# Sliding-window attention with a two-layer MLP: tile 0's attention moved ahead of the weights, its masks added as scores on TensorE, its layer one in wide products

## The chip, the cores and the metric

The kernel runs on one core of a Trainium2 chip. A core has five engines with a queue of instructions each: TensorE (PE, matrix products and transposes into PSUM), VectorE (DVE), ScalarE (ACT), GpSimd (POOL) and SyncE (SP). Loads and stores run on 16 DMA engines; here POOL issues all loads, SP the stores and the transposes done by DMA. The metric is the device time of one execution in microseconds (us). "The profile" is one execution recorded instruction by instruction, with times from the span's start.

## The reference

```python
scores = scale * np.matmul(q, k.transpose(0, 1, 3, 2))     # 8 batches, 8 heads, 576 tokens, 64 wide
mask = np.abs(pos[:, None] - pos[None, :]) <= 32
scores = np.where(mask, scores, -1000000000.0)
attn = softmax(scores)                                     # over the last axis
x = (attn @ v) with the heads side by side                 # 4608 tokens x 512
h = x @ w_in                                               # w_in 512 x 2048
g = h * (1.0 / (1.0 + np.exp(-1.702 * h)))
out = g @ w_out                                            # w_out 2048 x 512, float32
```

Inputs are float32 in HBM; loads convert q, k, v to bf16 and the weights to f16.

## The kernel before, in words

The 4608 tokens are 36 units of 128 queries, and nine tiles of four units (512 tokens). Everything is written out in program order; nothing is scheduled by a planner. An engine runs its queue in that order, so a waiting instruction holds up what stands behind it.

Attention of a unit: `scores` (24 small products into two PSUM banks, then two exponentials on ACT, into p), `band` (L257, DVE multiplies p by a 0/1 mask), `values` (16 pairs of products p by v, with a column of ones that gives the sums), `norm` (DVE: reciprocal and product, giving x), `x_T` or `x_T2` (PE transposes x for one or two units, and a copy brings it to xT). The odd half-blocks of v lie shifted by 64 tokens in `vo`, which `odd_v` (L200) copies from two neighbouring `ve` tiles, two copies a unit.

Layer one of tile 0 is done directly by `layer1_plain` (L377), layer two by `layer2_plain` (64 products of 512 columns, handed out a few at a time by `do(self.l2, n)`). Tiles 1 to 8 use a Strassen-like scheme with seven products in place of eight (`l1_group`, `layer2`), fed by sums of weights (`w1_sums`, `w2_sums`), of x and of g that DVE makes.

`opening` (L561) is tile 0, and the attention of tile 1. It loads k and q of tile 0 in two parts (`load_first`, `T_first`), k and q of tile 1 together (`load_four`, `T_four`: 32 PE transposes and two copies each), v by units (`load_v`, unit 4 in two halves), w_in in four chunks of 512 columns (`load_w1`) and w_out in four chunks of 512 rows (`load_w2`). All of these are issues on POOL's queue, and the n-th waits on the semaphore of the load eight before it. The loads' order before: k and q part 0, v0 to v2, w_in 0, k and q part 1, w_in 1, v3, half of v4, w_in 2, half of v4, tile 1's k and q, w_in 3, v5, v6, w_out 0, v7, v8, w_out 1 to 3, then tile 2's loads (`fetch`).

PE's order before: units 0 and 1 with `keep_busy` (products on a zero tile whose results nobody reads) in between, then transposes of part 1 mixed with layer one on the first half of the tokens, units 2 and 3, more layer one, tile 1's transposes, scores and values of units 4 to 7 mixed with the rest of layer one and 24 of the layer-two products. After it come `x_sums(1)` and `first_layer1`, tile 1's layer one.

PSUM has eight banks, all named: A, C, B, E, LA, LB and the double bank t. Taking a bank waits until its last reader is done. ACT needs another table for exponentials than for the gelu; each switch is an `ACT_TABLE_LOAD`.

Of the kernel before, what the change touches and what calls it, by code (L numbers as in the profile page):

```python
# [22 lines left out]
SQ = 64  # L23
TILE = 512


class _Kernel:
# [7 lines left out]
    def __init__(self, ctx, tc, q, k, v, w_in, w_out, out):  # L35
# [18 lines left out]
        self.g, self.gs, self.o = {}, {}, {}  # L54
# [28 lines left out]
    def setup(self):  # L83
# [3 lines left out]
        self.mask = cst.tile([128, 4, SQ], BF16, name="mask")  # L87
        self.w1 = cst.tile([128, 4, self.DFF], F16, name="w1")
# [10 lines left out]
    def setup_mask(self):  # L99
        pool, m = self.nc.gpsimd, self.mask  # L100
        lo, hi = slice(0, 64), slice(64, 128)
        pool.memset(m, 1.0)
        for blks, rows, sign in ((slice(0, 2), lo, 1), (slice(0, 2), hi, -1), (slice(2, 4), lo, -1), (slice(2, 4), hi, 1)):
            ap = m[rows, blks, :]
            pool.affine_select(out=ap, in_=ap, compare_op=ALU.is_ge, fill=0.0, base=0,
                               pattern=[[0, 2], [-sign, SQ]], channel_multiplier=sign)

    def cut_mask(self):
        lo, hi = slice(0, 64), slice(64, 128)
        for b, rows, cols in ((0, hi, slice(0, 32)), (0, lo, slice(32, 64)), (2, lo, slice(0, 32)), (2, hi, slice(32, 64))):  # L110
            self.nc.gpsimd.memset(self.mask[rows, b, cols], 0.0)

    def load_w1(self, c, n=1):
        w = 512 * n
        self.nc.gpsimd.dma_start(self.w1[:, :, c * 512:c * 512 + w],  # L115
                                 self.w_in[:, c * 512:c * 512 + w].rearrange("(k p) f -> p k f", p=128))
# [39 lines left out]
    def T_first(self, c, part, tags, engs):  # L156
# [6 lines left out]
        for i, (tag, eng) in enumerate(zip(tags, engs)):  # L163
            tp = self.bank(tag, [128, 2, j, n // j], BF16, "tp")
            for h in range(4):
                for x in range(j):
                    self.nc.tensor.transpose(tp[64 * (h % 2):64 * (h % 2) + 64, h // 2, x, :],
                                             src[:, 4 * i + h, at + x, :], self.ident[r, r])
            self.copy(eng, dst[:, 2 * i:2 * i + 2, :].rearrange("x h (p j) -> x h p j", j=j),
                      tp.rearrange("x h j p -> x h p j"))  # L170
# [66 lines left out]
    def scores(self, u, tag):  # L237
        kT, q = self.kT[u], self.qT[u]
        nxt = self.k_first if u == self.NU - 1 else self.kT[u + 1][:, :, 0:64]
        if tag == "t":  # L240
            sc = self.bank(tag, name="sc")
            sc = [sc[:, 0], sc[:, 1]]
        else:
            sc = [self.bank(x, name="sc") for x in tag]
        for hp in range(4):
            c = 128 * hp
            for eo in range(2):
                r = slice(64 * eo, 64 * eo + 64)
                lo, hi = sc[eo][0:64], sc[eo][64:128]
                self.mm(lo[:, c:c + 64], kT[r, hp, 0:64], q[r, hp, 0:64], start=(hp == 0))  # L250
                self.mm(hi[:, c:c + 128], kT[r, hp, 64:128], q[r, hp, :], start=(hp == 0))
# [125 lines left out]
    def layer1_plain(self, t, d, half, tag, later=None):  # L377
# [3 lines left out]
        c = slice(256 * half, 256 * half + 256)  # L381
        for i in range(2):
            f = 2 * d + i
            for kr in range(4):
                self.mm(h[:, 256 * i:256 * i + 256], self.w1[:, kr, 128 * f:128 * f + 128], self.xT[t][:, kr, c],
                        start=(i == 0 and kr == 0))

        def gelu():
            self.nc.scalar.activation(g[:, 2 * d:2 * d + 2, c], h.rearrange("p (i n) -> p i n", i=2),
                                      AF.Gelu_apprx_sigmoid)  # L390
# [170 lines left out]
    def opening(self):  # L561

        nc, dve, act, pool = self.nc, self.nc.vector, self.nc.scalar, self.nc.gpsimd
        self.setup()
        dve.memset(self.idle, 0.0)
        dve.memset(self.spark, 0.0)
        for t in self.ve:
            dve.memset(t[:, :, self.D:], 1.0)
        self.load_first("k", 0)
        self.load_first("q", 0)  # L570
        make_identity(nc, self.ident)
        act.activation(self.spark, self.spark, AF.Exp)
        for u in (0, 1, 2):
            self.load_v(u)
        self.load_w1(0)
        self.setup_mask()
        self.load_first("k", 1)
        self.load_first("q", 1)
        self.cut_mask()
        self.load_w1(1)  # L580
        self.load_v(3)
        self.load_v(4, slice(0, 1))
        self.load_w1(2)
        self.load_v(4, slice(1, 2))
        self.load_four("k")
        self.load_four("q")
        self.load_w1(3)
        dve.tensor_copy(self.identh, self.ident)
        self.keep_busy(10, "E", 512)
        self.T_first("k", 0, "AC", (dve, act))  # L590
        self.keep_busy(2, "E", 512)
        self.T_first("q", 0, ("LA", "LB"), (dve, act))
        self.keep_busy(1, "E", 512)
        for u in (5, 6):
            self.load_v(u)
        self.load_w2(0)
        for u in (7, 8):
            self.load_v(u)
        for c in (1, 2, 3):
            self.load_w2(c)  # L600
        self.load_kq("k", 8)
        self.scores(0, "t")
        self.scores(1, "AC")
        self.odd_v(0, dve)
        self.odd_v(1, dve)
        self.keep_busy(4, "E", 512)
        self.band(0)
        self.values(0, "t")
        self.band(1)
        self.norm(0)  # L610
        self.values(1, "AC")
        self.norm(1)
        self.keep_busy(2, "E", 512)
        self.x_T(0, "LA", act)
        self.keep_busy(1, "E", 512)
        self.x_T(1, "LB", act)
        self.T_first("k", 1, "AC", (dve, dve))
        h, n, gelus = [], [0], []

        def l1(half, *ds):  # L620
            for d in ds:
                self.layer1_plain(0, d, half, h[n[0] % len(h)])
                n[0] += 1

        self.layer1_plain(0, 0, 0, "B", gelus)
        self.T_first("q", 1, ("LA", "LB"), (dve, act))
        self.layer1_plain(0, 1, 0, "E", gelus)
        self.odd_v(2, dve)
        self.odd_v(3, dve, (0,))
        h[:] = ["B", "E", "LA", "LB"]  # L630
# [281 lines left out]
```

## Time and profile before

| what | us |
|---|---|
| median of 3 runs (285.96 to 287.16) | 287.05 |
| the profiled execution itself | 285.75 |
| its span, first to last instruction | 284.0 |
| PE busy in the span | 272.8 (96%) |
| DVE busy | 217.2 (76%) |
| ACT busy | 193.9 (68%) |
| POOL busy | 126.9 (45%) |

Rows of the profile give engine, line, operation, output<-input with shapes, and count. A busy PE is not always a useful one: products on the zero tile count as busy. Names in rows: `w` is w_in or w_out in SBUF, `h` layer one's result in PSUM, `o` layer two's, `sc` scores, `pv` values, `tp` a transpose in PSUM, `kq` the k and q of tile 0 or their transposes, `o_sb<-in_k_dram` the k of tile 1 (its buffer is shared with later outputs), `ve` and `vo` the v blocks, `junk` the products on zeros. Line 70 is the helper through which all products go.

### The profile page before, as it was taken

To read this page: it belongs to the slowest core of one execution; us is meant where nothing else is said; L and a number is where in the kernel's file an instruction comes from. 1 tells how busy PE (TensorE), PEld (TensorE's weight loads), DVE (VectorE), ACT (ScalarE), POOL (GpSimd) and SP (SyncE) were. 2 spreads that over 40 slices of the span, in tenths; PEclk is the share of its full clock that TensorE was granted. 3 is DMA by queue.
4 is the path that set the end of the run, shared out by engine and by line. 5 is a ranking of instruction groups with operands and counts; after the bars stand their busy time and mean duration, and the time that the engine had idled before them with its cause. 6 is when DMAs were issued, how large, how long until landed. Compare 5 with 4: busy or idle time off the path is not lost.

```text
span 284.0 us, 8953 instructions
## 1 busy us (share of the span) xinstructions
PE 272.8 (96%) x3684; PEld 223.3 (79%) x3684; DVE 217.2 (76%) x501; ACT 193.9 (68%) x340; POOL 126.9 (45%) x192
## 2 busy tenths in 40 slices
PE   6787999999999998999999999999999999999995
PEld 2466847776778887888888888888888888888884
DVE  1754997898887877798879887878788878946731
ACT  2556684799886778667966796689658875568411
POOL 8975446898599726739083909340110000000000
PEclk9999999999999999999999999999999999999999
DMA  8999999999999999999999999995422030201024
GB/s 90 182 193 196 184 204 159 193 124 147 136 154 152 200 127 195 124 203 143 201 102 189 131 203 82 198 146 140 132 58 71 26 113 14 81 2 74 2 95 133
DMA packets 149610, 37.63 MB, mean 132 GB/s; under 512 B 138048, under 2 KB 145216, under 8 KB 149568
## 3 DMA queue, kind: packets, MB, share of 16 engines
q0 software_dynamic: 106000, 18.42, 95.0%
q1 hardware_dynamic: 43120, 18.10, 34.2%
q8 instruction: 29, 0.48, 0.7%
q10 hardware_dynamic: 448, 0.52, 0.6%
q14 instruction: 13, 0.11, 0.1%
HBM read 36.83 MB, written 9.44 MB: 163 GB/s over the span
## 4 chain that ended last, share of the span: by engine, by line
PE 82%; DMA 7%; DVE 5%; POOL 4%; issue 1%; ACT 0%; DVEq 0%; POOLq 0%
PE o L70 37%; PE h L70 36%; PE pv L70 4%; DMA w<-in_moe_w_in_dram 4%; DMA xT<-x 3%; PE sc L70 3%; POOL ve L198 1%; POOL kq L142 1%; DVE xs L353 1%; DVE vo L209 1%; PE tp L321 1%; PE tp L231 1%; DVE a L334 1%; PE tp L188 1%; POOL w L115 1%
## 5 line engine op out<-in xcount | busy, mean ns | idle before, releaser
L418 ACT ACTIVATE g<-h 128x512 f16<-128x512 f32 x128 | 72.2, 598 | 35.7 <-PE h L70 34.9
L70 PEld LDWEIGHTS <-g 128*128 128x128 f16 x576 | 54.4, 98 | 9.5
L70 PEld LDWEIGHTS <-a 128*128 128x128 f16 x512 | 49.1, 97 | 12.3 <-DVE xs L353 2.2
L70 PE MATMUL h<-xs,a 128*128 128x256 f16 x384 | 57.6, 272 | 0.9 <-DVE xs L353 0.7
L70 PE MATMUL o<-w,g 128*128 128x256 f16 (+1 forms) x320 | 55.5, 294 | 0.0
L70 PEld LDWEIGHTS <-w 128*128 128x128 f16 x512 | 48.9, 98 | 8.4 <-DMA w<-in_moe_w_in_dram 1.7
L70 PE MATMUL h<-xT,w 128*128 128x256 f16 x384 | 54.0, 273 | 1.4 <-DMA w<-in_moe_w_in_dram 1.4
L209 POOL COPY vo<-ve 64x264 int32<-64x264 int32 x55 | 25.5, 463 | 61.3 <-PE pv L70 59.0
L70 PEld LDWEIGHTS <-gs 128*128 128x128 f16 x384 | 36.8, 98 | 4.7
L255 ACT ACTIVATE p<-sc 128x512 bf16<-128x512 f32 x72 | 36.9, 620 | 2.6 <-PE sc L70 2.5
L70 PE MATMUL o<-b,gs 128*128 128x256 f16 x256 | 37.6, 273 | 0.0
L70 PE MATMUL o<-b,g 128*128 128x256 f16 x256 | 37.5, 273 | 0.0
L198 POOL DMA_DIRECT2D ve<-in_v_dram x40 | 34.4, 865 | 6.2 <-DMA qst<-in_q_dram 2.8
L431 DVE TENSOR_TENSOR h<-h,s 128x512 f32<-128x512 f32 x32 | 22.3, 698 | 17.8 <-PE h L70 17.5
L131 POOL DMA_DIRECT2D qst<-in_q_dram x35 | 28.1, 804 | 3.5 <-DMA w<-in_moe_w_out_dram 2.8
L67 ACT COPY h<-h 128x512 f32<-128x512 f32 x32 | 18.9, 589 | 15.5 <-PE h L70 15.1
L293 DVE TENSOR_TENSOR x<-pv,rec 128x256 f16<-128x256 f32 (+1 forms) x53 | 27.6, 520 | 1.8
L131 POOL DMA_DIRECT2D kst<-in_k_dram x31 | 26.4, 855 | 5.0 <-DMA ve<-in_v_dram 2.6
L437 DVE TENSOR_TENSOR h<-h,s 128x512 f32<-128x512 f32 x32 | 22.4, 700 | 4.6 <-PE h L70 3.9
L263 DVE TENSOR_TENSOR p<-p,mask 128x1024 bf16<-128x1024 bf16 x36 | 25.0, 698 | 0.8 <-ACT p L255 0.6
L67 ACT COPY s<-h 128x512 f32<-128x512 f32 x32 | 19.2, 599 | 2.0 <-PE h L70 0.7
L70 PE MATMUL h<-xs,w 128*128 128x256 f16 x128 | 19.2, 273 | 0.0
(83 smaller groups left out, 343.7 us busy)
## 6 DMA issues: line engine op xcount, KB each, us to landing
out_dram<-o_sb SPq DMA_DIRECT2D x33, 256.0 KB, 4.6
ve<-in_v_dram POOLq DMA_DIRECT2D x32, 128.0 KB, 6.6
kst<-in_k_dram POOLq DMA_DIRECT2D x25, 128.0 KB, 6.6
qst<-in_q_dram POOLq DMA_DIRECT2D x21, 128.0 KB, 6.1
w<-in_moe_w_in_dram POOLq DMA_DIRECT2D x4, 512.0 KB, 8.9
w<-in_moe_w_out_dram POOLq DMA_DIRECT2D x4, 512.0 KB, 12.6
qst<-in_q_dram POOLq DMA_DIRECT2D x7, 96.0 KB, 6.4
kq<-in_q_dram POOLq DMA_DIRECT2D x2, 256.0 KB, 5.9
```

The source lines that it names most:

```text
L67: (eng.copy if eng is self.nc.scalar else eng.tensor_copy)(out, in_)
L70: self.nc.tensor.matmul(out, lhsT, rhs, start=start, stop=stop, skip_group_check=True)
L115: self.nc.gpsimd.dma_start(self.w1[:, :, c * 512:c * 512 + w], self.w_in[:, c * 512:c * 512 + w].rearrange("(k p) f -> p k f", p=128))
L131: self.nc.gpsimd.dma_start(t[off:off + n], src[b, :, s:s + n, :].rearrange("h s d -> s h d"))
L198: self.nc.gpsimd.dma_start(t[off:off + n, :, :self.D], self.v[b, :, s:s + n, :].rearrange("h s d -> s h d"))
L209: eng.tensor_copy(*((words(vo[64:128]), words(self.ve[u % 9][64:128])), (words(vo[0:64]), words(nxt)))[i])
L255: self.nc.scalar.activation(p[:, eo].rearrange("k h s -> k (h s)"), sc[eo], AF.Exp, scale=self.scale)
L263: (eng or self.nc.vector).tensor_mul(pv, pv, msk.to_broadcast([128, 8, 2, SQ]))
L293: dve.tensor_mul(x[:, 4 * at:4 * (at + n), :].rearrange("p (b h) d -> p b h d", b=n), acc[:, :, :, :D], r.to_broadcast([128, n, 4, D]))
L418: act.activation(g[:, f, 256 * half:256 * half + 256], bank.rearrange("p (i n) -> p i n", i=2), AF.Gelu_apprx_sigmoid)
L431: dve.tensor_add(e, b, s7)
L437: dve.tensor_add(c, b, s7)
```

## The change

Seven things, all but the last two in `opening`:

- The loads' order becomes k and q of tile 0 (both parts), v0 to v3, half of v4, w_in 0 and 1, then on POOL eight `odd_v` copies, then w_in 2, tile 1's k and q, w_in 3, the rest of v4, v5 to v8, w_out 0 to 3, eight more `odd_v` copies, and then tile 2's loads. The sixteen copies ran on DVE before.
- The identity matrices and the mask are made on DVE from one iota on POOL; they were made on POOL.
- For units 0 to 3, `seed` writes 0 or -1e8 into the two score banks by a product of the identity and a bias tile, and the score products add to it; the exponential then gives zero outside the band, and `band` is not called.
- Attention of units 0 to 3 is done whole before layer one begins. The zero products are 24 of 128 columns, 12 of 256, and 8 of 64, in place of 20 of 512.
- Layer one of tile 0 is done for two pairs of column blocks in halves of 256 tokens, for the other twelve blocks in products of 512 tokens. Two of these blocks are copied by DVE from PSUM to SBUF and their gelu taken from there; the gelus of blocks 10 to 15 are called after the exponentials of units 4 to 7. Again 24 of the layer-two products are called in `opening`, in groups of 4, 4, 8 and 8.
- Unit 10 and 11's transposes of x become two `x_T`, copied by DVE and ACT, instead of one `x_T2` copied by DVE.
- One `w1_sums` of the second half moves from `opening` into `first_layer1`.

```diff
...
     def setup_mask(self):
-        pool, m = self.nc.gpsimd, self.mask
-        lo, hi = slice(0, 64), slice(64, 128)
-        pool.memset(m, 1.0)
...
+        D = self.work.tile([128, 128], F32, name="gap", tag="s7", bufs=2)
+        self.nc.gpsimd.iota(D, pattern=[[-1, 128]], base=0, channel_multiplier=1,
+                            allow_small_or_imprecise_dtypes=True)
+        dve = self.nc.vector
+        dve.tensor_single_scalar(self.ident, D, 0.0, op=ALU.is_equal)
+        dve.tensor_copy(self.identh, self.ident)
...
+                dve.tensor_single_scalar(self.mask[r, blk:blk + 2, :], d, 0.0, op=op)
...
+    def setup_bias(self):
+        m = self.mask[:, 1:4:2, :].rearrange("p (o b) s -> p o b s", o=1).to_broadcast([128, 4, 2, SQ])
+        self.nc.vector.tensor_scalar(out=self.bias.rearrange("p (o b s) -> p o b s", o=4, b=2), in0=m, scalar1=-1.0,
+                                     scalar2=1.0e8, op0=ALU.add, op1=ALU.mult)
...
+    def seed(self, u, tag):
+        self.sc[u] = self.score_banks(tag)
+        for x in self.sc[u]:
+            self.mm(x, self.ident, self.bias, start=True)
...
+    def scores(self, u, tag=None):
...
+        bias = tag is None
+        sc = self.sc.pop(u) if bias else self.score_banks(tag)
         for hp in range(4):
             c = 128 * hp
+            start = hp == 0 and not bias
...
+    def layer1_plain(self, t, f, half, tag, later=None, eng=None):
...
+        fs, c = ((f, f + 1), slice(256 * half, 256 * half + 256)) if half is not None else ((f,), slice(0, TILE))
+        w = TILE // len(fs)
+        for i, f1 in enumerate(fs):
             for kr in range(4):
+                self.mm(h[:, w * i:w * i + w], self.w1[:, kr, 128 * f1:128 * f1 + 128], self.xT[t][:, kr, c],
                         start=(i == 0 and kr == 0))
+        if eng:
+            kept = self.sb("s7", [128, 512], F32, 2)
+            self.copy(eng, kept, h)
+            h = kept
...
```

The new body of `opening`, after the two loads of part 0 and the setup:

```python
self.load_first("k", 1); self.load_first("q", 1)
act.activation(self.spark, self.spark, AF.Exp)
for u in (0, 1, 2, 3): self.load_v(u)
self.load_v(4, slice(0, 1))
self.load_w1(0); self.load_w1(512)
for u in (0, 1, 2, 3): self.odd_v(u, pool)
self.load_w1(1024)
self.load_four("k"); self.load_four("q")
self.load_w1(1536)
self.load_v(4, slice(1, 2))
for u in (5, 6, 7, 8): self.load_v(u)
for c in range(4): self.load_w2(c)
self.keep_busy(24, "E", 128); self.keep_busy(12, "E")
self.T_first("k", 0, "AC", (dve, act)); self.seed(0, "t")
self.T_first("q", 0, ("LA", "LB"), (dve, act)); self.seed(1, "AC")
self.scores(0); self.scores(1)
self.T_first("k", 1, ("LA", "LB"), (dve, dve)); self.T_first("q", 1, ("B", "E"), (dve, act))
self.seed(2, "t"); self.seed(3, "AC")
self.keep_busy(8, "LA", 64)
self.scores(2); self.scores(3)
self.values(0, ("LA", "LB")); self.norm(0)
self.values(1, ("B", "E")); self.norm(1)
self.x_T(0, "LA", act)
self.values(2, "t"); self.norm(2)
self.x_T(1, "LB", act)
self.values(3, "AC"); self.norm(3)
self.x_T(2, "B", act)
h, n = ["LA", "LB", "A", "C", "B", "E"], [0]
l1(0, 0)
self.x_T(3, "E", dve)
l1(0, 2); l1(1, 0, 2)
...
l1(None, 4, 5, 6, 7, 8)
for i in (3, 1, 2, 4): self.w1_sums((i,), 0)
...
self.T_four("k", "BE", (dve, act))
...
l1(None, 9)
self.T_four("q", "BE", (dve, act))
for u in (4, 5, 6, 7): self.odd_v(u, pool)
self.load_kq("k", 8)
for u in (8, 9, 10, 11): self.fetch(u)
l1(None, 10, later=gelus, eng=dve)
self.scores(4, "AC"); self.scores(5, "t"); self.scores(6, "BE")
l1(None, 11, later=gelus, eng=dve)
self.scores(7, "AC"); self.band(4); self.band(5)
l1(None, 12, later=gelus); self.values(4, "t")
l1(None, 13, later=gelus); self.band(6); self.norm(4)
l1(None, 14, later=gelus); self.values(5, "AC"); self.band(7)
l1(None, 15, later=gelus); self.norm(5)
self.values(6, "t")
self.do(gelus[2:4] + gelus[0:2] + gelus[4:])
self.norm(6)
self.do(self.l2, 4)
self.values(7, "AC"); self.norm(7)
self.do(self.l2, 4)
self.x_T2(4, "t", act)
self.do(self.l2, 8)
self.x_T2(6, "A", dve)
self.do(self.l2, 8)
```

Later in `run` and in `first_layer1`:

```diff
-        self.x_T2(10, "C", dve)
+        self.x_T(10, "A", dve)
+        self.x_T(11, "C", act)
...
-        dv = [lambda i=i: self.w1_sums((i,), 1) for i in (1, 2, 4)]
+        dv = [lambda i=i: self.w1_sums((i,), 1) for i in (3, 1, 2, 4)]
```

More of the change, by code (lines that the diff above doesn't have):

```diff
@@ L87, in setup @@
         self.mask = cst.tile([128, 4, SQ], BF16, name="mask")
+        self.bias = cst.tile([128, 512], BF16, name="bias")
         self.w1 = cst.tile([128, 4, self.DFF], F16, name="w1")
@@ L564, in opening @@
         self.setup()
+        self.load_first("k", 0)
+        self.load_first("q", 0)
         dve.memset(self.idle, 0.0)
         dve.memset(self.spark, 0.0)
+        self.setup_mask()
+        self.cut_mask()
+        self.setup_bias()
         for t in self.ve:
             dve.memset(t[:, :, self.D:], 1.0)
[L569 to L574, printed above, removed]
@@ L592, in opening @@
         self.T_first("q", 0, ("LA", "LB"), (dve, act))
[L593 to L608, printed above, removed]
@@ L614, in opening @@
         self.x_T(0, "LA", act)
[L615 to L628, printed above, removed]
```

173 lines of the change are left out of this document (86 added, 87 removed).

## The prediction

> **What bounds the kernel now.** I read the view by slices first, then stretches of ten microseconds, then the timeline of the opening. From 50 us on, TensorE (PE) is busy without a break and the change hardly touches it, so the opening is what can move. In this table each row is a stretch, followed by the busy time of PE, weight load, VectorE (DVE), ScalarE (ACT), GpSimd (POOL), and at the end GB/s of DMA:
>
> ```profile
> 0.00:10.00 10.00, 7.51 (x121) 3.75 (x121) 3.11 (x17) 3.58 (x6) 8.55 (x19) 1.00 1.24 112
> 10.00:20.00 10.00, 7.82 (x153) 5.37 (x152) 6.32 (x15) 4.66 (x10) 8.02 (x15) 1.00 1.56 192
> 20.00:30.00 10.00, 8.12 (x124) 6.63 (x122) 6.25 (x15) 6.45 (x11) 5.61 (x7) 1.00 1.45 197
> 30.00:40.00 10.00, 9.55 (x206) 6.82 (x205) 9.30 (x18) 8.95 (x15) 5.04 (x8) 1.00 1.61 191
> 40.00:50.00 10.00, 9.98 (x102) 6.57 (x102) 8.32 (x22) 5.56 (x9) 6.12 (x8) 1.00 1.99 170
> ```
>
> PE idles 6.55 us in the first 30 us (2.49 + 2.18 + 1.88), and the groups add 6.8 us of products on the zero tile, which compute nothing. In the same time DMA runs at an even 190 to 200 GB/s: the loads are in one saturated stream, and each lands when all loads ahead of it have. The timeline shows when (start, length, work, and in brackets the wait before it):
>
> ```profile
> 1.27 3.78 PE L70 MATMUL junk<-idle 128*128 128x512 bf16 x10 [1.27 <-DVE spark L566]
> 6.81 0.60 PE L70 MATMUL junk<-idle 128*128 128x512 bf16 x2
> 23.44 1.05 PE L70 MATMUL h<-xT,w 128*128 128x256 f16 x8 [1.24 <-DMA w<-in_moe_w_in_dram]
> 29.28 0.74 POOL L119 DMA_DIRECT2D w<-in_moe_w_out_dram  x1 [1.14 <-DMA o_sb<-in_q_dram]
> 30.46 1.11 PE L188 MATMUL tp<-ident,o_sb 128*64 128x128 bf16 x32
> 31.67 0.74 POOL L119 DMA_DIRECT2D w<-in_moe_w_out_dram  x1 [1.66 <-DMA w<-in_moe_w_in_dram]
> 34.08 1.28 ACT L255 ACT_TABLE_LOAD   x1
> 35.37 4.03 ACT L255 ACTIVATE p<-sc 128x512 bf16<-128x512 f32 x8
> 39.88 0.87 POOL L131 DMA_DIRECT2D qst<-in_q_dram  x1 [1.25 <-DMA w<-in_moe_w_out_dram]
> 42.45 0.87 POOL L131 DMA_DIRECT2D kst<-in_k_dram  x1 [1.69 <-DMA w<-in_moe_w_out_dram]
> 47.06 0.60 PE L70 MATMUL h<-xT,w 128*128 128x256 f16 x4
> ```
>
> A POOL load waits for the eighth load before it to land, so POOL's waits date the landings: third w_in chunk 23.4, tile 1's q 29.2, fourth w_in chunk 31.6, second and third w_out chunk 39.8 and 42.4. A 512 KB weight chunk takes 2.4 us of the stream (29.28 to 31.67), a 128 KB load of v some 0.85 (a wait at 35.66 ends on w_out, the next at 36.52 on v), the first 256 KB of q about 1.45 (PE starts k at 6.01, q at 7.43). The last line is my mark: the first product of tile 1's layer one, at 47.06. Both kernels have issued 24 of tile 0's 64 layer-two products by then, and what follows is the same but for two trifles. The time moves by what the mark moves.
>
> **Loads.** The new order puts all of tile 0's k, q, v first, then three w_in chunks, tile 1's k and q, the fourth w_in chunk, half a v, v5 to v8, w_out. The first w_in chunk has ahead of it what the second had (18.7), less a chunk (2.4), plus 192 KB of v (1.25): 17.5 instead of some 12.5 (issued at 6.21, and no w load landed under 6.3 after its issue). The third has exactly the same set as before: 23.4. Tile 1's k and q come without 64 KB of v: 0.35 earlier, 26.1 and 28.9. w_out's second and third chunks stay at 39.8 and 42.4.
>
> **Attention of tile 0.** Its v land from 11.1 (7.4 + 2 x 1.45 for k, q, + 0.85) by 0.85 each, the last half at 14.1. The shifted copies go from DVE (0.29) to POOL (row: 0.40 median), eight of them, chained behind the second v at 12.0: done near 15, just ahead of the issue of w_in's third chunk. Normalising two banks took 1.17 (12.74 to 13.91), so units 1 to 3 end near 15.8, 16.7 and 18. Thus attention ends as the first weights land: that part of the change does what it says. The eight seeds of the mask (8 x 0.217, from eight 512-wide products in 1.90) are 1.7 us of new PE work in time in which PE has nothing else. The four masks on DVE (0.69 each) go; the setup of ident, mask and bias on DVE is bounded by 0.2 (cast, 128x128) and 0.82 (copy, 128x640) each, some 2.5 us for all, and is done before the first copy is due at 6.6; at the upper bound that copy is 1 to 2 us late, but the v at 12 hide it. POOL's iota (nearest row: 0.29, a 128x128 select) hides behind k and q in the stream.
>
> **Layer one.** Wide or half, the columns are equal: eight 256-wide products take 0.87, four 512-wide 4 x 0.217 = 0.87. The wide products save nothing on PE. From 17.5: nine such groups and one transposition of x (0.35) reach tile 1's k at 25.7, which lands at 26.1; 32 transpositions 1.05 (30.46 to 31.51), one group, and PE stands at tile 1's q at 28.1, 0.8 before it has landed (before: 30.46, 1.2 after). So the head start is cut by the stream.
>
> **From tile 1's q to the mark.** Before: 31.51 to 47.06 is 15.55, with 0.45 idle (0.30 and 0.15 in front of values), so 15.1 of work. After has the same left: six groups of layer one, scores and values of four units, 24 products of layer two, two x transpositions. 28.9 + 1.05 + 15.1 = 45.1. The new waits:
> - Scores of unit 4 wait for q's copies with one group of 0.87 as cover. Before, the ACT copy ended 2.17 after the transpositions began (30.46 to 32.63); PE is free 1.9 after: 0.3 idle.
> - ACT's table load (1.28) comes behind these scores, then two exponentials (1.0, from 4.03 for eight) free banks A and C for scores of unit 7: 31.6 + 1.3 + 1.0 = 33.9, plus 0.15. PE has scores of 5 and 6 and one group as cover, to 33.0: 1.0 idle.
> - Layer two's banks LA, LB come free after eight exponentials (36.9), a table load (38.2) and two gelus (39.4); PE is there at 39.4: 0.1. The two gelus moved behind DVE copies are not due before the last eight products.
> - POOL's copies for units 4 to 7 start after the last w_out issue (32.5) and end near 36.5; values need them from 35.3 on, one unit per 1.4: nothing, and a copy of 0.94 (the longest) still just fits. Tile 2's loads queue behind these copies until 37, but the stream is full with w_out until 45.
>
> Sum: 45.1 + 1.4 = 46.5, the mark 0.6 earlier. Behind it, one w_sum more on DVE (0.68, DVE 9.2 of 10 busy there) and unit 11's x copy on ACT instead of DVE: each between -0.2 and +0.3, taken as 0, since PE waited only 0.7 us in all for DVE after the opening. The profiled execution took 285.75 (span 284.0 and 1.75 around it), 1.3 under the median of the runs, 287.05: 285.15 on its own scale, **286.4** on that of the median. 0.5%, or 1.4 us, is about what a measurement tells from no change.
>
> **Rivals.**
> A, faster: loads land 1 us sooner, or the new waits are covered, ACT being ready sooner than I chain it. PE then runs through: 27.65 + 1.05 + 15.1 = 43.8. But the first product after the 24 needs w_out's last chunk (42.4 + 2.5 = 44.9), which is due 0.4 after the mark: 44.5, 2.5 earlier: 284.5. For it: PE is the only bound there if the stream gives way. Against: the stream shows no gap to win.
>
> B, slower: POOL's eight copies stand ahead of six loads. If each takes 0.94 (longest row) from 11.1 on, w_in's third chunk is issued at 18.6. At the shortest landing of a w load, 6.3, or the page's median, 8.9, it lands at 24.9 or 27.5 instead of 23.4, and all behind it as late, 287.9 to 290.5, middle 289.2. It decides from an issue at 17.7 on (23.4 - 6.3 + my 0.6), which is 0.82 per copy. Against: the median is 0.40, with DVE three quarters busy. The Trainium skill, page "SBUF — State Buffer", section "Who interferes with whom", says that a GpSimd operation blocks for the whole of a DVE operation with two SBUF inputs or in a two-port mode; by that rule copies near 0.94 are possible, though DVE mostly reads PSUM between 11 and 15. The trace has such copies among its 55, but does not show what held them.
>
> C, about even: without the zero products of 9 to 13 us, PE does too little before 17.5 and drops to the rate of the start, 0.42 per 512 columns (3.78 for ten) instead of 0.217; fast again were the two at 6.81, so 3.8 to 5.5 us, costing 1.85 to 2.65 less the 1.25 of slack before q: 287.0 to 287.8. Against: no gap there exceeds 1.2 us, and before stood as long (22.2 to 23.44) without harm. The Trainium skill, page "TensorE: Matmul & The Clock Gate", section "HAM oscillation — how this bites in real kernels", asks for an idle window of some 3.4 us before PE slows; by that rule C is unlikely. The trace agrees as far as its 1.24 us gap goes.
>
> **Numbers.** Forecast 0.48 (own range 285.4 to 288.0 for 0.5 us of landing and of waits either way and the spread of runs; at its ends 0.05 beyond the bound on either side), A 0.21, B 0.20 (0.18 beyond the bound), C 0.11 (0.01 beyond). Faster 0.05 + 0.21 = 0.26; slower 0.05 + 0.18 + 0.01 = 0.24; same 0.50. The range reaches to A's 284.5 and B's middle, 284.4 to 289.2.
>
> **What will show it.** First layer-one product near 17.5 with little PE idle from there to 28; a PE wait of about 0.8 before tile 1's q, one of about 1 before scores of unit 7; third w_in chunk issued near 15; mark at 46.5. Wrong if q lands off 28.9 by over 1 us, if POOL's copies exceed 0.6, or if 512 columns take 0.42 after 17.5.

## The result, and the profile after

The changed kernel takes 288.16 us (median of 20 executions, 286.86 to 289.95) against 286.13 for the kernel before (20 executions, 285.36 to 287.16): a ratio of 1.0069, interval 1.0050 to 1.0087. It is 2.0 us slower. The prediction had 286.4 and "same" as the likeliest outcome; it was reckoned as 0.6 us under the 287.05 of the three runs known then, which on the 286.13 of these twenty would be 285.5. The execution profiled after took 289.35 (span 287.6), 1.2 over its median, the one before 285.75, 0.4 under its own. So the two traces lie 3.6 us apart where the medians lie 2.0 apart; 1.5 of that comes behind the last product (a store issued by ACT took 2.03 us there against 0.48). I read the traces for places, and take sizes from medians.

The five stretches of the opening, after (columns as in the prediction):

```profile
0.00:10.00 10.00, 8.60 (x160) 6.60 (x160) 4.72 (x25) 3.72 (x6) 8.87 (x16) 1.00 1.15 116
10.00:20.00 10.00, 7.54 (x173) 5.75 (x174) 6.46 (x20) 6.87 (x12) 7.03 (x14) 1.00 1.65 179
20.00:30.00 10.00, 8.22 (x73) 4.59 (x71) 4.52 (x8) 6.75 (x12) 5.78 (x8) 1.00 1.34 185
30.00:40.00 10.00, 9.09 (x184) 4.99 (x184) 6.81 (x13) 8.26 (x13) 7.62 (x12) 1.00 1.68 187
40.00:50.00 10.00, 9.98 (x96) 6.09 (x96) 5.59 (x14) 5.19 (x9) 8.47 (x11) 1.00 1.85 177
```

DVE is relieved as the change says (28.1 busy of 50 us). The new thing is in the last column: the loads move 179 and 185 GB/s from 10 to 30 us, where it was 192 and 197. The timeline of the same execution shows why, and where it was felt:

```profile
11.82 0.40 POOL L223 COPY vo<-ve 64x264 int32<-64x264 int32 x1 [1.11 <-DMA ve<-in_v_dram]
12.64 0.86 POOL L223 COPY vo<-ve 64x264 int32<-64x264 int32 x2 [0.42 <-DMA ve<-in_v_dram]
14.65 2.25 POOL L223 COPY vo<-ve 64x264 int32<-64x264 int32 x5 [1.15 <-DMA ve<-in_v_dram]
16.85 0.74 POOL L126 DMA_DIRECT2D w<-in_moe_w_in_dram  x1
17.94 1.04 PE L70 MATMUL h<-xT,w 128*128 128x256 f16 x8
26.73 1.11 PE L202 MATMUL tp<-ident,o_sb 128*64 128x128 bf16 x32 [0.59 <-DMA o_sb<-in_k_dram]
30.13 1.05 PE L202 MATMUL tp<-ident,o_sb 128*64 128x128 bf16 x31 [1.32 <-DMA o_sb<-in_q_dram]
34.66 0.24 PE L70 MATMUL sc<-kq 64*64 64x64 bf16 x3 [0.54 <-ACT p L291]
47.03 0.60 PE L70 MATMUL h<-xT,w 128*128 128x256 f16 x4
73.91 0.39 PE L70 MATMUL o<-b,g 128*128 128x256 f16 x2 [0.63 <-DVE g L402]
100.60 2.81 SPq L341 DMA_TRANSPOSE xT<-x  x2
111.51 0.43 DVE L389 TENSOR_TENSOR xs<-xT 128x512 f16<-128x512 f16 x1 [2.65 <-DMA xT<-x]
111.99 0.61 PE L70 MATMUL h<-xs,a 128*128 128x256 f16 x4 [1.28 <-DVE xs L389]
```

POOL's eight copies wait for v and hold the third w_in chunk and all loads behind it until 16.85; tile 1's q lands at 30.1; the mark is at 47.03, level with 47.06 before. From there the changed kernel loses: 0.63 at 73.9 for DVE, then at 112 for the x of tile 3, which DMA transposes. The same place in the kernel before, by its timeline:

```profile
98.91 3.16 SPq L305 DMA_TRANSPOSE xT<-x  x2
106.42 0.70 PE L70 MATMUL sc<-qT,kT 64*64 64x64 bf16 x48
109.61 0.42 DVE L353 TENSOR_TENSOR xs<-xT 128x512 f16<-128x512 f16 x1 [1.45 <-DMA xT<-x]
110.09 0.61 PE L70 MATMUL h<-xs,a 128*128 128x256 f16 x4 [0.69 <-DVE xs L353]
```

PE waits there in the kernel before too: x of units 14 and 15 is handed to the DMA queue at 98.91 and lands 10.7 us later, and PE is 0.69 early. After, SP hands it over at 100.60 and it lands at 111.5. I call the landing of this x the floor: behind it come products of PE, near 110, that cannot start before it.

### The profile page after: what moved, and what is told of

It reads as the page before. It is cut to its first block, busy times and chain, and to the rows that moved or that the text cites. A ratio compares the mean times of both kernels' runs of the same rounds, so it can differ in the third digit from the quotient of the medians.

```text
span 287.6 us, 8929 instructions
## 1 busy us (share of the span) xinstructions
PE 273.8 (95%) x3668; PEld 222.3 (77%) x3668; DVE 213.0 (74%) x494; ACT 196.1 (68%) x343; POOL 133.1 (46%) x198
## 4 chain that ended last, share of the span: by engine, by line
PE 78%; DMA 9%; POOL 4%; DVE 3%; ACT 2%; issue 2%; ACTq 1%; POOLq 0%; DVEq 0%
PE o L70 35%; PE h L70 35%; PE pv L70 4%; DMA o_sb<-in_q_dram 4%; DMA xT<-x 3%; PE sc L70 3%; DMA ve<-in_v_dram 2%; POOL kq L153 1%; POOL ve L212 1%; DVE xs L389 1%; ACT p L291 1%; ACTq L504 1%; PE tp L245 1%; ACT g L461 1%; ACT L291 1%
## 5 line engine op out<-in xcount | busy, mean ns | idle before, releaser
L223 POOL COPY vo<-ve 64x264 int32<-64x264 int32 x71 | 34.0, 479 | 65.0 <-PE pv L70 59.2
L70 PE MATMUL h<-xT,w 128*128 128x256 f16 (+1 forms) x336 | 53.7, 288 | 0.0
L70 PEld LDWEIGHTS <-w 128*128 128x128 f16 x464 | 44.4, 98 | 9.5
L67 ACT COPY h<-h 128x512 f32<-128x512 f32 x32 | 18.8, 586 | 17.7 <-PE h L70 17.3
L299 DVE TENSOR_TENSOR p<-p,mask 128x1024 bf16<-128x1024 bf16 x32 | 22.4, 701 | 1.4 <-ACT p L291 1.4
L67 ACT COPY o_sb<-o 128x256 f32<-128x256 f32 (+1 forms) x23 | 10.7, 465 | 13.1 <-PE o L70 8.7
```

The source lines that it names most:

```text
L67: (eng.copy if eng is self.nc.scalar else eng.tensor_copy)(out, in_)
L70: self.nc.tensor.matmul(out, lhsT, rhs, start=start, stop=stop, skip_group_check=True)
L223: eng.tensor_copy(*((words(vo[64:128]), words(self.ve[u % 9][64:128])), (words(vo[0:64]), words(nxt)))[i])
L299: (eng or self.nc.vector).tensor_mul(pv, pv, msk.to_broadcast([128, 8, 2, SQ]))
```

## The experiments

"Before" was measured again with each set: 286.36, 286.36, 286.33, 286.20 and 286.22. Ratios are to the runs of before with the same set, with a 95% interval behind them.

**The two late edits.** One kernel with only `w1_sums` put back, one with both late edits put back (the new opening alone), one with the late edits alone on the kernel before.

```diff
-for i in (3, 1, 2, 4)]                 # first_layer1
+for i in (1, 2, 4)]
+self.w1_sums((3,), 1)                  # back in opening, after layer two's groups
-self.x_T(10, "A", dve); self.x_T(11, "C", act)     # second kernel
+self.x_T2(10, "C", dve)
```

> The changed kernel with the moved w_sum put back into the opening, ahead of x's transposes of units 4 and 5. Theory 1 (the extra DVE operation in tile 1's layer one pushes the update of g behind two masks, and PE waits 0.63 us for it at 73.9): that wait is gone, tile 2's first product comes 0.6 to 0.8 us earlier than in the changed kernel (82.0 there), total 0.4 to 0.8 us faster than it. Rival (DVE is behind because the opening leaves it behind, whatever is in the list): the wait on g stays, no change.

> The changed kernel with both later edits taken back: the w_sum, and one transposition and copy for units 10 and 11 in place of two. Only the opening is new. Theory 1: about the time of the kernel before, within 0.5 us, since both openings reach tile 1's first product at 47.0. Rival (the new opening leaves the loads of tile 2 and 3 later, and the x transposes by DMA at 105 to 112 pay for it): still 0.8 to 1.2 us slower than before, with a DVE wait of over 2 us for xT near 110.

> The kernel before with the two later edits alone: the w_sum moved into tile 1's layer one, and two transpositions and copies for units 10 and 11. Theory 1: 0.5 to 1.0 us slower than before, with the PE wait on g near 73 and 0.15 us lost in front of tile 2. Rival (all comes from the opening): no change.

Measured: 288.39 (1.0072, 1.0042 to 1.0101), 288.12 (1.0058, 1.0022 to 1.0093), and 287.11 (1.0031, 1.0010 to 1.0052). On the old opening the late edits cost 0.75 us, and the trace of that kernel has the wait that the changed kernel has:

```profile
73.70 0.39 PE L70 MATMUL o<-b,g 128*128 128x256 f16 x2 [0.63 <-DVE g L366]
```

The sum of weights (0.68 on DVE) pushes the update of g behind two bands: it runs at 73.2 (73.4 in the changed kernel) and not at 69.7. With only `w1_sums` put back the wait for g is gone from the trace, and the time stays; taking both edits out of the changed kernel gains nothing that can be measured either. What is gained ahead of 105 us is lost at 110:

```profile
106.37 0.44 PE L70 MATMUL sc<-qT,kT 64*64 64x64 bf16 x22 [0.33 <-DMA kT<-kst]
110.86 0.61 PE L70 MATMUL h<-xs,a 128*128 128x256 f16 x4 [1.76 <-DVE xs L389]
```

This is the new opening alone. Its mark came at 46.05, a whole microsecond ahead of the kernel before, and at 105.5 it was still 0.9 ahead; at 110.86 it is 0.8 behind.

**POOL's copies on DVE.** In the changed kernel, the eight `odd_v` copies of units 0 to 3.

```diff
-for u in (0, 1, 2, 3): self.odd_v(u, pool)
+self.odd_v(0, dve); self.odd_v(1, dve)   # ahead of values(0); 2 and 3 behind norm(0) and norm(1)
```

> The changed kernel with the shifted copies of units 0 to 3 on DVE, as before, so that POOL issues the third w_in chunk without waiting for v. Theory: the dip in DMA throughput from 18 to 23 us (140 to 182 GB/s in the changed kernel) goes, tile 1's q lands at 28.9 instead of 30.1, the mark (tile 1's first product of layer one) moves from 47.03 to 46.0 or a little later, total 0.6 to 1.1 us faster than the changed kernel. Rival (the dip has another cause, or w_out's stream decides the mark): q lands at 30 as before and the mark stays within 0.3.

Measured: 289.22 (1.0103, 1.0063 to 1.0142, six executions), slower still. Yet the dip of the load stream was gone (4.65 MB moved by 28 us, against 4.40 in the changed kernel and 4.61 before). What had taken its place was TensorE's clock: 0.982 to 0.994 as a mean over these executions; in the profiled one, the shortest of the six (286.53), 0.61 from 18 to 22 us, and the first layer-one product at 19.28 with 1.91 us for the eight that take 1.04. Two causes were mixed here, so they were taken apart below.

**x of units 14 and 15 by TensorE.** This removes the place where the lead is lost: eight transposes on PE (0.44 us at 101.06) in place of two on the DMA queue; done to the new opening alone, to the kernel before, and to the changed kernel as it stands.

```diff
 # in back(2): the last two x_T(u) without a bank (DMA) go, and in fill() of the fourth group:
+if t == 2 and n == 3 and i == 2:
+    self.x_T2(14, "t", self.nc.scalar)
```

> The new opening alone (both late edits undone), and x of units 14 and 15 transposed by TensorE (8 products, about 0.6 us) instead of by DMA. Theory one, a floor at 110 us: the DMA transpositions of these units land behind the queued loads, and eat whatever the opening won (the new opening alone was 0.9 us ahead of the kernel before at 106.4 and 0.8 behind it at 110.9, with a wait of 1.76 for DVE's differences of x). Then that wait falls under 0.3, PE ends near 280.5 instead of 281.64, and the median comes 1.0 to 1.3 under that of the new opening alone: about 287.0. Theory two, the floor is of the whole load stream and only changes its face (kT of unit 17, loads of tile 3): another DMA wait of 1 us or more shows up between 106 and 116, and the median stays at 288.0.

> The kernel before with the same edit: x of units 14 and 15 by TensorE. Theory one: its wait at 110 was 0.69 and goes, the 8 transpositions cost 0.6, so it stays within 0.3 of the kernel before (286.1 to 286.6). Theory two: the same or up to 0.6 slower, as the wait turns up elsewhere.

> The changed kernel as it stands, both late edits in, with x of units 14 and 15 transposed by TensorE. If the floor at 110 us took what the opening won, it falls as the new opening alone did with this edit (288.12 to 285.98). The late edits, which the floor hid until now (the new opening with and without them: 288.16 and 288.12), should then show with the 0.6 to 0.75 that they cost on top of the kernel before (287.11 against 286.36): 286.6 to 286.7. If the late edits cost nothing in the new opening: 286.0. If the floor is not the cause: 287.5 or more.

Measured: 285.98 (1.0002, 0.9977 to 1.0028), 286.45 (0.9999, 0.9978 to 1.0021) and 286.46 (1.0012, 0.9992 to 1.0032). The same edit is worth 2.1 us to the new opening and 1.7 to the changed kernel by the medians (1.6 to both by the ratios), and nothing to the kernel before. In the timeline of the first, PE goes through 110 without the wait:

```profile
107.35 0.44 PE L70 MATMUL sc<-qT,kT 64*64 64x64 bf16 x22 [0.28 <-DMA kT<-kst]
109.48 0.60 PE L70 MATMUL o<-w,g 128*128 128x256 f16 x4
109.91 0.60 PE L70 MATMUL h<-xs,a 128*128 128x256 f16 x4
```

With the floor gone the late edits also show: 286.46 against 285.98.

**The clock.** In 8 of the 20 executions of the changed kernel the mean granted clock was 0.990 to 0.996; in the other kernels that have the new opening with its eight zero products of 64 columns the mean was under 0.997 in 57 of 73, in the kernel before in 28 of 146. The changed kernel was given products on zeros of 256 columns in PE's gaps.

```diff
+self.keep_busy(4, "B")      # ahead of T_first("q", 1)
-self.keep_busy(8, "LA", 64)
+self.keep_busy(8, "LA")
+self.keep_busy(6, "LB")     # between scores(2) and scores(3); 3 each ahead of values(1),
+                            # behind x_T(0) and behind x_T(1)
```

> The changed kernel with about 2.5 us of products on the zero tile (256 columns) put into PE's gaps between 9 and 17.5 us. If the drop of the granted clock near 15 to 22 us (mean clock 0.990 to 0.996 in 8 of 20 executions) is a small matter, as the executions with it were only 0.3 us longer than those without: all executions at 0.998 or more, median 287.7 to 288.0. If it is the main loss (rival C): 287.0 or less. If the products get in the way of the attention: first layer-one product later than 18.2 and the median above 288.4.

Measured: 287.84 (1.0054, 1.0030 to 1.0078), every execution at 0.999 or 1.000: the products do hold the clock up, and the time hardly moves. The same products in the new opening alone, in a later set:

> The new opening alone (late edits undone) with the products on the zero tile that hold the clock up; copies of v for units 0 to 3 on POOL, x of units 14 and 15 by DMA. The base of the pair. By the theory of the late stream: 0.1 to 0.2 MB behind at 28 us, tile 3's x lands at 110.3 to 111.5, PE waits 1.5 or more for it, median 287.5 to 288.0.

Measured: 287.31 (1.0036, 1.0012 to 1.0060), a little under the forecast, against 1.0058 without them. With x by TensorE the same pair is 285.98 without (above) and 286.19 with them (below). So by the medians the clock costs 0.6 us at most as long as POOL makes the copies; the intervals overlap, so more is not excluded. With the copies on DVE it may cost more: 289.22 without these products, 286.85 with them and without the late edits (below). By stretches, the new opening alone without these products, then the changed kernel with them:

```profile
12.00:16.00 4.00, 2.30 (x90) 1.62 (x86) 1.37 (x6) 2.17 (x4) 2.36 (x6) 0.95 1.74 187
16.00:20.00 4.00, 4.00 (x57) 3.20 (x56) 2.83 (x10) 2.71 (x4) 3.94 (x7) 0.62 1.22 196
```

```profile
12.00:16.00 4.00, 3.89 (x98) 2.84 (x96) 0.75 (x4) 2.17 (x4) 2.30 (x7) 1.00 1.75 184
16.00:20.00 4.00, 3.87 (x70) 2.98 (x65) 3.41 (x12) 2.27 (x4) 3.94 (x7) 1.00 1.18 192
```

**Why the floor itself lies later.** Tile 3's x lands at 109.6 in the kernel before and at 110.3 to 112.9 behind the new opening with POOL's copies, also where PE is earlier. Of two guesses the first failed and the second was not settled. First, the late issue of tile 2's loads (39.9 in place of 32.4), by taking the copies of units 4 to 7 off POOL:

```diff
-for u in (4, 5, 6, 7): self.odd_v(u, pool)
+self.odd_v(4, dve)          # 5, 6 and 7 on DVE among the bands
```

> The changed kernel with the shifted copies of v for units 4 to 7 on DVE (eight of 0.29) instead of POOL, so that tile 2's loads are issued from 34.2 instead of 39.9. If that late issue is what puts the load stream behind (0.17 to 0.24 MB less than in the kernel before from 40 to 52 us, at 155 GB/s 1.1 to 1.5 us): the gap is closed by 48, tile 3's x lands 0.7 to 1 earlier, median 287.2 to 287.5. If the stream fell behind at 16 to 28 already, through the copies of units 0 to 3 and their late issue of the third w_in chunk: the gap stays, median 288.2.

Measured: 288.40 (1.0073, 1.0043 to 1.0103); the stream was 0.17 MB behind at 52 us (8.75 against 8.92 MB), little less than without the edit (8.72), and x landed at 112.7. Second, the loads that stand right ahead of the transpositions, by moving the last fetch behind POOL's copies of unit 19:

```diff
-self.fetch(u + n + 6)       # for n == 3 of back(2) now behind odd_v(u + n + 4)
```

> The new opening alone, DMA transpositions kept, but the last fetch of that stretch (q of unit 20, k and v of unit 21) issued by POOL behind the copies of unit 19, which wait for PE at about 98: these 384 KB (2.5 us at 155 GB/s) then stand behind the transpositions of x and not ahead of them. If queued loads are what makes the transpositions take 8 to 11 us: x lands 1.5 to 2.5 us earlier, the wait of 1.76 falls under 0.5, median 286.5 to 287.2. If the transpositions are slow by themselves or wait for each other: x lands at 110 as before, median 288.1.

Measured: 288.90 (1.0079, 1.0052 to 1.0106), x at 112.85. Moving three loads does not move x forward. But the edit moved their issues from 92 to 95 us to 100 to 102, and two of the three still went ahead of the hand-over of x (101.28), so it does not settle whether queued loads slow the transpositions. From the stretches 0 to 28 us, the last column separates the kernels. In order the kernel before, the changed kernel, and one with the copies on DVE and the clock held up (next run):

```profile
0.00:28.00 28.00, 21.45 (x363) 13.98 (x365) 13.95 (x44) 14.11 (x24) 21.32 (x38) 1.00 1.42 165
```

```profile
0.00:28.00 28.00, 23.56 (x402) 16.74 (x402) 14.63 (x49) 15.90 (x27) 20.66 (x34) 1.00 1.38 157
```

```profile
0.00:28.00 28.00, 24.91 (x385) 17.74 (x387) 16.51 (x56) 15.04 (x25) 18.60 (x27) 1.00 1.41 166
```

165 against 157 GB/s over 28 us is 0.2 MB, 1.3 us of a stream that carries some 157 GB/s from 44 to 100 us. In every trace with a deficit of 0.1 to 0.26 MB at 28 us nearly all of it is still there at 52. The landings sort by it: 109.1 to 110.2 in the five kernels with 4.61 MB or more by 28 us and x by DMA, 110.3 to 112.9 in the eight with some 4.5 or less. That is one execution of each kernel: the five were profiled in executions 0.1 to 2.7 us under their medians, five of the eight in executions 0.6 to 1.8 over theirs. So the order alone does not show that the stream sets the landing.

Between stream and landing lies SP's queue. From x of unit 13 on (88.5 to 90.6 us) it issues, with no pause over 0.1 us in the four traces below, a store in two parts, two pairs of q and k, and then x of unit 14; one transposition takes it 1.2 to 2.8 us. The table has when DVE has made unit 14's x, when SP hands it over, and when DVE reads the landed pair:

| kernel | MB by 28 us | x made | handed over | pair read |
|---|---|---|---|---|
| before | 4.61 | 98.88 | 98.91 | 109.61 |
| changed | 4.40 | 99.68 | 100.60 | 111.51 |
| new opening alone | 4.5 | 97.99 | 99.29 | 110.38 |
| split copies, x by DMA (below) | 4.65 | 97.54 | 98.82 | 109.05 |

In the kernel before, SP takes x as soon as it is made, and its queue had been busy until 98.68: there was 0.2 us of slack. A lead in making x is lost in this queue: 1.3 us earlier made, 0.1 earlier handed over in the last row. Of the changed kernel's 1.9 us at the landing, 0.8 is x made later, 0.9 the wait in the queue, 0.2 the transposition. Earlier, SP waits for q and k to land (12.4 us from 56 to 76 in the changed kernel, 9.8 before), but these waits do not tell a late stream from a whole one: 12.5 in the split version, 9.6 in the kernel before with a stalled stream (below). How the stream's deficit reaches x is not shown.

> The same with the copies of units 0 to 3 on DVE (eight of 0.29). Theory of the late stream: 4.60 MB or more moved by 28 us, as in the kernel before, tile 3's x lands at 109.6 to 110.2, median 286.3 to 286.8, about the kernel before, since the transpositions by DMA still end any lead. Rival, the stream of the opening has no part in what happens at 110 us: x lands as in the run with the copies on POOL, median within 0.4 of it.

> The same with the copies on DVE, and x of units 14 and 15 by TensorE: neither fault left. If both theories hold, the mark near 46.3 comes through to the end: 285.3 to 285.7, the only version under both kernels. The version with the copies on POOL took 286.19, with a wait of 0.52 for kT of unit 15 near 81 and tile 1's q at 30.04; if these were chance and not the stream, 286.0 to 286.3.

> The kernel before with ten memsets on POOL (128x256, 0.36 each by the mask's) ahead of the issue of w_in's third chunk, which comes at 16.9 instead of 13.27, as in the changed kernel (16.85). Theory of the late stream: 0.1 to 0.2 MB behind at 28 us, tile 3's x lands at 110.3 to 111.5 instead of 109.6, 0.7 to 1.9 us slower, 287.1 to 288.2; part of it may show as waits for w_in and tile 1's q before 32. Rival, the stream catches up: the deficit is gone by 52 us, x lands at 109.6, and the time differs only by what the mark has moved.

The three edits: the warm opening above with the copies on DVE; that with x by TensorE; and, on the kernel before,

```diff
+for _ in range(10): pool.memset(self.spare, 0.0)
 self.load_w1(2)
```

Measured: 286.85 (1.0015, 0.9994 to 1.0035), 286.42 (0.9997, 0.9971 to 1.0023) and 287.33 (1.0046, 1.0028 to 1.0064). With the stream whole, x lands at 110.1 instead of 111.8 (this is the first of the three, then its base with POOL's copies, in an execution 1.4 over its median; by the medians the two are 0.5 apart, within the noise):

```profile
110.09 0.42 DVE L389 TENSOR_TENSOR xs<-xT 128x512 f16<-128x512 f16 x1 [1.89 <-DMA xT<-x]
110.57 0.61 PE L70 MATMUL h<-xs,a 128*128 128x256 f16 x4 [0.88 <-DVE xs L389]
```

```profile
111.80 0.42 DVE L389 TENSOR_TENSOR xs<-xT 128x512 f16<-128x512 f16 x1 [3.17 <-DMA xT<-x]
112.28 0.61 PE L70 MATMUL h<-xs,a 128*128 128x256 f16 x4 [1.70 <-DVE xs L389]
```

The second missed its 285.3 to 285.7: with all copies on DVE and so many zero products the first layer-one product comes at 20.15, the mark at 47.2, and there is no lead to carry (its profiled execution, 289.98, was 3.6 over its median). The third shows that the old opening, stalled on POOL alone, also falls to 4.36 MB at 28 us, has not caught up by 52, and costs 1.1 us (x at 111.2). But its PE is 1.35 late at the mark too, through waits for w_out, and makes unit 14's x 1.4 later, so it does not separate paying there from paying at the floor.

**Copies split.** Copies of units 0 and 1 on DVE, which idles from 11.9 to 14.5; those of 2 and 3 on POOL, but behind the issues of w_in's third chunk and of tile 1's k; fewer zero products; late edits out; with x of units 14 and 15 by TensorE and by DMA.

```diff
+self.load_w1(1024)
+self.load_four("k")
+for u in (2, 3): self.odd_v(u, pool)
-for u in (0, 1, 2, 3): self.odd_v(u, pool)
-self.load_w1(1024); self.load_four("k")
 self.load_four("q")
...
+self.odd_v(0, dve); self.odd_v(1, dve)
 self.values(0, ("LA", "LB"))
```

> The new opening alone, copies of units 0 and 1 on DVE (idle there from 11.9 to 14.5), those of units 2 and 3 on POOL behind the issues of w_in's third chunk and of tile 1's k, fewer products on the zero tile, x of units 14 and 15 by TensorE. Theory: 4.6 MB by 28 us, first layer-one product near 18.7, tile 1's q without a wait near 29.0, mark at 46.0, no wait at 110: 285.0 to 285.6, under the kernel before (286.2) by 0.6 or more. If a lead of 1 us is lost again, another wait on the stream (kT of unit 15 or 17) takes it and the median is 286.0 to 286.4.

> The same with x of units 14 and 15 transposed by DMA. Theory: x lands at 109.6 to 110.2 whatever the lead, PE waits 1.5 or more for it, median 286.2 to 286.7, 0.6 to 1.2 above the run with TensorE's transpositions. If the lead got through by itself once the stream is whole: 285.5 or less.

Measured: **284.94** (0.9958, 0.9937 to 0.9978) and 286.09 (1.0001, 0.9978 to 1.0025). The first beats both kernels, by 1.3 and 3.2 us. In the second x landed at 109.05, not at 109.6 or later as forecast: 0.6 us of the lead got through there, PE waited 0.43 for it and 0.82 for kT of unit 17 ahead of it, and at the end nothing was left. The timeline of the first has no wait at tile 1's q, the mark 1.4 us earlier than before, and no wait at 108 to 110:

```profile
28.77 1.11 PE L202 MATMUL tp<-ident,o_sb 128*64 128x128 bf16 x32
45.70 0.60 PE L70 MATMUL h<-xT,w 128*128 128x256 f16 x4
105.56 0.70 PE L70 MATMUL sc<-qT,kT 64*64 64x64 bf16 x48
108.38 0.60 PE L70 MATMUL h<-xs,a 128*128 128x256 f16 x4
```

**The masks.** The run with warm products, POOL's copies and x by TensorE, and the same with the masks of units 0 to 3 multiplied in by DVE.

```diff
-self.seed(u, tag)
-self.scores(u)
+self.scores(u, tag)
+self.band(u)                # ahead of values(u), u = 0 to 3
```

> The new opening alone, x of units 14 and 15 by TensorE, and the products on the zero tile in PE's gaps between 9 and 17.5 us, which held the granted clock at 0.999 or more in the changed kernel. There its mark came at 45.95 against 46.81 in the run with x by TensorE and no such products. With no floor behind it, half to all of these 0.86 us should reach the end: 285.1 to 285.6, clearly under the kernel before (286.36). If a second floor lies behind the first (kT of unit 17 by DMA, which already waited 0.28 there): 286.0, no better than without.

> The run with warm products and x by TensorE, with the masks of units 0 to 3 multiplied in by DVE (four of 0.69) instead of seeded by TensorE (eight products of 0.22 in idle time). This is the part of the change that speaks of masks, undone alone. If the 2.8 us of DVE work lie in the chain of attention, units 2 and 3 end 1.4 to 2.8 later, tile 0's layer one starts up to 1.4 later, and part of it comes through: 0.4 to 1.0 above the run with seeds. If tile 1's q (28.9 to 30.1) covers it: the same within 0.3.

Measured: 286.19 (1.0001, 0.9977 to 1.0024) and 289.29 (1.0108, 1.0087 to 1.0128). The masks on TensorE are worth 3.1 us in this opening (five executions), far more than I gave them. As bands, they come one by one between the norms in DVE's queue, and PE waits 1.57, 1.10 and 0.97 us for three of them; tile 0's layer one starts at 22.30 instead of 18.67. The clock drops as well (eight products take 1.92; the mean is 0.987 to 0.994 in all five), so a part of the 3.1 is the clock's. Another order of the bands was not tried.

```profile
22.30 1.92 PE L70 MATMUL h<-xT,w 128*128 128x256 f16 x8
```

The first of the two fell short of its own 285.1 to 285.6: the stream still late, PE waits 1.14 for tile 1's q (30.04) and 0.52 for kT of unit 15 at 81.6.

These runs give a square of medians, from three sets, all with the late edits out and the clock held up (the split opening has fewer zero products):

| | x of 14, 15 by DMA | x of 14, 15 by TensorE |
|---|---|---|
| copies on POOL ahead of the loads | 287.31 | 286.19 |
| copies split, loads not held up | 286.09 | 284.94 |

Holding up the loads costs 1.2 us in both columns, and the DMA transpositions of x cost 1.1 in both rows; by the ratios it is 1.0 to 1.2, each give or take some 1.0. In the right column the 1.2 is paid at tile 1's q (30.04 against 28.77).

## Why the prediction was wrong

The direction was wrong: 2.0 us slower where no change was forecast. The step that failed first is the sentence "The time moves by what the mark moves", with the late edits "taken as 0" behind it. The mark at 47.03 was level with before, 0.5 later than the 46.5 forecast and inside its margin, and the time was 2.0 longer. The premise was that PE, busy without a break from 50 us on, sets the pace, so that all that follows shifts with the mark. The trace of before shows DVE waiting 1.45 us at 109.6 for a DMA transposition and PE 0.69 behind it; I counted this as "only 0.7 us in all for DVE", a small wait, when it meant that the chain behind it (x made, handed over by SP, transposed) had only 0.2 us of slack left. A lead of 1.3 us in making x hardly passed it in the split version, and in the changed kernel PE waits 1.28 there.

Point by point:

- *Loads, even stream.* First layer-one product 17.94 for 17.5: right. Tile 1's q at 30.1 for 28.9: wrong by more than the 1 us that I had named as the test. I let v land one by one, every 0.85 us, and had the copies done near 15 and the third w_in chunk issued then. Measured, five of the eight copies waited for v until 14.65 and the issue came at 16.85. From 10.7 to 16.85 POOL issued no load, and the stream moved 140 to 182 GB/s from 18 to 23 us in the changed kernel (175 to 207 before). The sum counted the loads' order and not this gap.
- *Attention ends as the first weights land; wide products cost the same.* Right: 7.10 us for 44 products of layer one from 19.04, PE without a break to 26.1. The masks as seeds: right in sign, and worth 3.1 us, the clock's part included, by the run without them.
- *The wait before scores of unit 7.* Forecast 1.0; two waits of 0.54 and 0.25.
- *Layer two and the mark.* 46.5 forecast, 47.03 measured; the 1.2 us of q is more than the difference. In the execution of the new opening alone that waited only 0.33 for q, the mark was at 46.05. From q to the mark it is 16.9 us both times, for 17.6 in the sum: this part was sound.
- *The late edits.* Taken as 0, with -0.2 to +0.3 each: measured 0.75 together on the old opening (interval 0.3 to 1.5), 0.3 to 0.5 on the changed kernel with the floor removed. The larger one is the wait of 0.63 for g.
- *Behind the mark.* Nothing forecast. Measured by the square above: 1.2 us through the held-up loads, where the traces show the waits at tile 1's q, at kT and at tile 3's x; and 1.1 for the lead of the opening that is taken away at 110.

Of the rivals, B named the right cause, POOL's copies ahead of six loads, but the wrong path: its condition (an issue later than 17.7, copies of 0.82) was not met, the copies took 0.40 to 0.45, and PE never waited for the third w_in chunk. The price goes with the bytes that the stream did not move. Of the rule from the Trainium skill, page "SBUF — State Buffer", section "Who interferes with whom", these eight copies show nothing: none was held up, they waited for v. Rival C happened in a part of the executions, though PE's longest gap in a trace with the drop was 1.27 us, hardly more than the 1.2 that I had counted against C; by the medians it costs 0.6 us at most, where I had 0.6 to 1.4. A did not happen in the changed kernel. The split version comes nearest to it, with no wait at q and the mark at 45.7 (A had 44.5), and even there the time is that of before (286.09) as long as x goes by DMA.

What stays open: why the transpositions of x of units 14 and 15 take 9.8 to 11.6 us from the hand-over to the landing of the pair in all thirteen traces (8.8 each in the kernel before, where the median of all 23 is 6.2); how a late stream reaches them; and which single executions of the changed kernel are long (they spread over 3.1 us; those of the split version with x by TensorE over 1.1). The clock explains it only in part: 12 of the 20 executions have no drop, and their spans run from 285.1 to 287.5.

## What to carry to other kernels

A small wait of a late stage for a DMA, in a kernel whose TensorE looks fully busy, can mark a place where a second chain has no slack: look there before crediting a gain in an early stage, and take that wait away together with the gain. Work on the queue that issues the loads can cost not its own time but what the stream doesn't move meanwhile; here the stream had not given it back by 52 us. Put the load issues first, or the work on an engine that idles. An edit that gains nothing can still be right: here three faults had to go before any of the opening's lead was seen.

## What the runs showed of the hardware

- The granted clock fell to half without a long pause of PE. In the new opening alone, PE's longest gap from 8.6 to 16 us was 1.27 us and PE was busy 5.9 of 8 us, and the clock read 0.95 and 0.62 in the two stretches shown: (0.05 + 0.38) x 4 = 1.7 us lost, which at half rate (eight products in 1.91 us for 1.04) would be one drop of 3.4 us by my estimate. The run with the copies on DVE gives the same (0.97 from 14 to 18, 0.61 from 18 to 22). The Trainium skill, page "TensorE: Matmul & The Clock Gate", section "HAM oscillation — how this bites in real kernels", warns of idle gaps of PE of over some 3.4 us. This trace does not agree: the clock fell without one. With products of 256 columns on zeros in these gaps, 3 of 84 executions had a mean clock under 0.997; with the eight of 64 columns that the changed kernel has there, 65 of 93. The kernel with the masks on DVE, whose PE waits longer, dropped in spite of them (5 of 5).
- The profile of the kernel before has as little PE work there (5.8 of 8 us, 8 to 16) and a clock of 1.00; its zero products were 512 columns wide. PE's busy time did not tell these two traces apart. The kernel before had a mean clock under 0.997 too, in 28 of 146 executions.
- A shortfall of 0.1 to 0.26 MB in the load stream at 28 us was found nearly whole again at 52 us in all traces that had one.
